# Switching to a transposing DMA one chunk earlier, with two scratch buffers per tensor and a reordered weight preparation

## The chip, the cores and the metric

The kernel runs on one core of one Trainium2 chip. The metric is the device time of that core in microseconds (us). A trace covers the span from the core's first to its last instruction, 1.7 to 2.2 us less than the device time in the runs of this study.

## The reference, cut to what matters

```python
# x, f_logit: 4 x 6144 x 256; w1, w2: 256 x 1024; w_out: 1024 x 256; all float32
sig = 1 / (1 + exp(-f_logit))
f = lower_bound + (1 - lower_bound) * sig
h = 0
for t in range(S):                    # a recurrence along the sequence
    h = f[:, t] * h + (1 - f[:, t]) * x[:, t]
    y[:, t] = h
out = maximum(y @ w1, y @ w2) @ w_out # 24576 tokens
```

## The kernel before

This kernel's matmuls take y with the feature dimension on the partitions, but f and x lie in memory with the tokens first. The sequence is cut into 26 chunks: four of 512 tokens at the start, then 22 of 1024. A block is 512 tokens, and there are 48. A chunk is turned in one of two ways. Early chunks are loaded with a cast to bf16 and transposed on TensorE. Later chunks are loaded into a DRAM scratch buffer with the same cast, and a transposing DMA brings them into SBUF.

```python
def by_xbar(c, s):                 # s = 0: f, s = 1: x
    return c >= (5, 6)[s]          # chunk index from which the DMA transposes
NSCR = 6                           # scratch buffers per tensor

def fetch(c):
    for s in range(2):
        ...                        # chunk 0 by the SyncE queue, cast on VectorE
        elif by_xbar(c, s):
            scr = scratch[s][uses[s] % NSCR]
            uses[s] += 1
            nc.gpsimd.dma_start(out=scr..., in_=src...)      # fp32 -> bf16
        else:
            nc.gpsimd.dma_start(out=nat..., in_=src...)      # to SBUF

def cross(c):
    for s in range(2):
        if by_xbar(c, s):
            nc.sync.dma_start_transpose(out=dst[:, :, 0:nt], in_=held[c, s][0:nt, :])
```

GpSimd does little but issue these loads, so it runs ahead of the computation until no scratch buffer is free: in the trace of before it issues them up to 40.81 us, and then waits 22.75 us for the first transposing DMA to free a buffer. SyncE issues the transposing DMAs and the outputs in program order.

The maximum is taken as a relu: wd is the scaled difference of w2 and w1, `first_layer` computes relu(wd.T y) with 16 matmuls of 512 columns, and `second_layer` multiplies that by w_out and adds y @ w13 with w13 = (scaled w1) @ w_out, 40 matmuls of 256 columns. The weight preparation before:

```python
def make_w1s(g):   # ScalarE: scaled copy of w1, fp32
    nc.scalar.mul(fcs(w1s, kc, g), half(w1n, g)[:, kc], om[:, kc:kc+1])
def make_wd(g):    # VectorE: w2 * om - w1s, 512 columns at a time
    nc.vector.scalar_tensor_tensor(out=fcs(wd, kc, g), in0=half(w2n, g)[:, kc], ...)
def make_w1T(k):   # TensorE transposes of w1s in fp32, ScalarE copies them to bf16
    ...
# order: make_w1s x2, make_wd(0), first_layer(0, 0..3), make_wd(1), make_w1T(0), (1),
#        first_layer(0, 4..7), make_w1T(2), (3), make_w13
```

The loop, cut to its order of work:

```python
LEAD_FETCH = 10; LEAD_CROSS = 3
for j in range(2, NBLK + 1):
    ahead("fetch", fetch, j + LEAD_FETCH)
    ahead("cross", cross, j + LEAD_CROSS)
    for fc in range(FC):
        if j < NBLK: first_layer(j, fc)
        second_layer(j - 1, fc)
        turn(...)          # TensorE transposes of block j + 2, if any
        ...                # gate (sigmoid) and scan of the next blocks
```

## Time and profile before

| what | value |
|---|---|
| device time, median of the first 3 runs | 409.04 us |
| span of the trace | 405.9 us |
| TensorE busy | 388.1 us, 96% |
| period of a block in the steady state | 7.82 us (48 blocks: 375 us) |
| first dense matmul stream | 14.05 us |
| first output matmul of block 0 | 23.92 us |
| first transposing DMA | issued 43.97, landed 63.5 us |

From the page of the kernel before: the busy times of the engines; the granted clock of TensorE and the mean busy share of the DMA engines in 40 slices of the span, in tenths; the chain of work that ended last, as shares by engine.

```profile
span 405.9 us, 7061 instructions
PE 388.1 (96%) x2792; PEld 297.3 (73%) x2840; DVE 247.2 (61%) x345; ACT 273.4 (67%) x446; POOL 28.0 (7%) x59
...
PEclk9999999999999999999999999999999999999999
DMA  7999999997999999897997995989772662752212
...
PE 82%; DMA 14%; issue 1%; SPq 0%; POOL 0%; ACT 0%; DVE 0%; ACTq 0%
```

TensorE is busy from end to end, and the chain is mostly TensorE. The DMA engines are full too for the first two thirds (mean share 0.85 to 1.20 in every stretch read between 10 and 300 us), but that alone does not say that anybody waited for them. Whether anybody did is in the list of what TensorE waited for (us in total, times, longest):

```profile
engine line waited for: us in total, times, longest us
PE dT L313 <- DVE wd L273: 5.6, 2, 5.2
PE tT L155 <- DVE fn L101: 2.8, 1, 2.8
...
PE dT L313 <- ACT rt L321: 1.2, 1, 1.2
```

The last line is a single wait of 1.2 us. The relus in front of it stood behind a sigmoid on ScalarE that had to wait for the first transposing DMA of f (2.7 us, until 63.6). SyncE's queue shows that DMA (start and duration of the issue):

```profile
...
30.05 13.82 SPq L365 DMA_DIRECT2D out_dram<-osb  x2
43.97 17.55 SPq L128 DMA_TRANSPOSE fT<-scr_0_90  x1
61.62 0.99 SPq L365 DMA_DIRECT2D out_dram<-osb  x2
```

Its issue alone took 17.55 us. The summary of the tile fT has its 19.6 us as the longest time from issue to landing:

```profile
DMA to landing us min/median/max: 4.7/5.9/19.6
```

The start, on TensorE alone (start, duration of the merged pieces, count):

```profile
start us, us, engine line op out<-in xcount [idle before <-releaser]
13.02 0.61 PE L313 MATMUL dT<-y,wd 128*128 128x512 bf16 x1 [5.17 <-DVE wd L273]
14.05 3.17 PE L313 MATMUL dT<-y,wd 128*128 128x512 bf16 x7 [0.42 <-DVE wd L273]
17.01 1.25 PE L287 MATMUL psO<-ident_f,w1s 128*128 128x128 f32 x8
18.09 1.98 PE L313 MATMUL dT<-y,wd 128*128 128x512 bf16 x8
...
20.79 2.41 PE L297 MATMUL psO<-wob,w1T 128*128 128x256 bf16 x16
...
23.92 0.27 PE L342 MATMUL psO<-w_117,y 128*128 128x256 bf16 x1
```

TensorE does nothing dense until 14.05. Then weight transposes (L287), the product w13 (L297) and transposes of block 1 (L155) stand between it and block 0's output matmuls (L342, at 23.92).

### The profile page before, as it was taken

To read this page: it belongs to the slowest core of one execution; us is meant where nothing else is said; L and a number is where in the kernel's file an instruction comes from. 1 tells how busy PE (TensorE), PEld (TensorE's weight loads), DVE (VectorE), ACT (ScalarE), POOL (GpSimd) and SP (SyncE) were. 2 spreads that over 40 slices of the span, in tenths; PEclk is the share of its full clock that TensorE was granted. 3 is DMA by queue.
4 is the path that set the end of the run, shared out by engine and by line. 5 is a ranking of instruction groups with operands and counts; after the bars stand their busy time and mean duration, and the time that the engine had idled before them with its cause. 6 is when DMAs were issued, how large, how long until landed. Compare 5 with 4: busy or idle time off the path is not lost.

```text
span 405.9 us, 7061 instructions
## 1 busy us (share of the span) xinstructions
PE 388.1 (96%) x2792; PEld 297.3 (73%) x2840; DVE 247.2 (61%) x345; ACT 273.4 (67%) x446; POOL 28.0 (7%) x59
## 2 busy tenths in 40 slices
PE   3699998999999999999999999999999999999996
PEld 2386776777777777777777777777777777777775
DVE  3557665676566567566656656756665665676641
ACT  2948655766766766676676677667667667766762
POOL 0721000000000000000000000000000000000000
PEclk9999999999999999999999999999999999999999
DMA  7999999997999999897997995989772662752212
GB/s 254 206 214 234 247 206 299 210 258 171 233 174 226 205 186 221 195 214 205 206 207 180 234 209 169 237 164 211 155 157 90 170 144 77 195 131 77 105 53 103
DMA packets 97568, 75.43 MB, mean 186 GB/s; under 512 B 87280, under 2 KB 87792, under 8 KB 96880
## 3 DMA queue, kind: packets, MB, share of 16 engines
q1 hardware_dynamic: 93984, 49.56, 47.7%
q0 software_dynamic: 3264, 25.17, 34.2%
q8 instruction: 22, 0.36, 0.4%
q10 hardware_dynamic: 288, 0.26, 0.2%
q14 instruction: 10, 0.08, 0.1%
HBM read 53.48 MB, written 46.66 MB: 247 GB/s over the span
## 4 chain that ended last, share of the span: by engine, by line
PE 82%; DMA 14%; issue 1%; SPq 0%; POOL 0%; ACT 0%; DVE 0%; ACTq 0%
PE psO L342 49%; PE dT L313 34%; DMA fT<-scr_0_90 5%; DMA scr_0_90<-in_f_logit_dram 4%; DMA scr_4_94<-in_f_logit_dram 3%; DMA w1n_118<-in_moe_w_dram 2%; DMA fn<-in_f_logit_dram 1%; POOL waited L269 0%; SPq L97 0%; ACT rt L321 0%; POOL wob L398 0%; SPq L380 0%; SPq L259 0%; DVE osb L351 0%; PE tT L155 0%
## 5 line engine op out<-in xcount | busy, mean ns | idle before, releaser
L321 ACT ACTIVATE rt<-dT 128x512 bf16<-128x512 f32 x384 | 223.3, 598 | 109.5 <-PE dT L313 93.4
L342 PE MATMUL psO<-wob,rt 128*128 128x256 bf16 x1536 | 229.1, 273 | 0.2
L313 PE MATMUL dT<-y,wd 128*128 128x512 bf16 x720 | 218.5, 382 | 6.9 <-DVE wd L273 5.6
L342 PEld LDWEIGHTS <-rt 128*128 128x128 bf16 x1536 | 170.0, 113 | 40.7
L362 DVE COPY osb<-psO 128x512 f32<-128x512 f32 x94 | 64.8, 691 | 76.2 <-PE psO L342 76.0
L208 DVE TENSOR_TENSOR_SCAN y<-ff,y,v 128x512 bf16<-128x512 bf16 x88 | 107.8, 1266 | 0.0
L313 PEld LDWEIGHTS <-wd 128*128 128x128 bf16 x768 | 73.9, 98 | 15.9 <-DVE wd L273 6.4
L342 PE MATMUL psO<-w_117,y 128*128 128x256 bf16 x384 | 73.3, 273 | 2.3
L342 PEld LDWEIGHTS <-y 128*128 128x128 bf16 x384 | 43.3, 113 | 41.0 <-issue 0.3
L195 DVE TENSOR_TENSOR v<-u,xT 128x1024 bf16<-128x1024 bf16 x40 | 27.7, 692 | 55.0 <-ACT u L165 55.0
L165 ACT ACTIVATE u<-fT 128x1024 bf16<-128x1024 bf16 x42 | 44.1, 1051 | 2.7 <-DMA fT<-scr_0_90 2.7
L184 DVE TENSOR_SCALAR ff<-u,nom 128x512 bf16<-128x512 bf16 x96 | 29.3, 347 | 0.0
L195 DVE TENSOR_TENSOR v<-u,tT 128x1024 bf16<-128x1024 bf16 x8 | 9.7, 1218 | 16.2 <-ACT u L165 14.9
L165 ACT ACTIVATE u<-tT 128x1024 bf16<-128x1024 bf16 x6 | 6.2, 1039 | 7.6 <-PE tT L155 7.5
L208 DVE TENSOR_TENSOR_SCAN y<-ff,v 128x512 bf16<-128x512 bf16 x8 | 9.3, 1206 | 0.0
L155 PE MATMUL tT<-ident,xn 128*128 128x128 bf16 x64 | 8.6, 230 | 0.3 <-DVE xn L101 0.3
L155 PE MATMUL tT<-ident,fn 128*128 128x128 bf16 x48 | 5.1, 234 | 2.8 <-DVE fn L101 2.8
L155 PEld LDWEIGHTS <-fn 128*128 128x128 bf16 x48 | 3.9, 105 | 3.5 <-DVE fn L101 3.1
L155 PEld LDWEIGHTS <-xn 128*128 128x128 bf16 x64 | 5.4, 103 | 0.6 <-DVE xn L101 0.6
L106 POOL DMA_DIRECT2D scr_0_90<-in_f_logit_dram x4 | 2.0, 496 | 50.0 <-DMA fT<-scr_0_90 49.4
L106 POOL DMA_DIRECT2D scr_2_92<-in_f_logit_dram x4 | 1.9, 487 | 37.0 <-DMA fT<-scr_2_92 36.2
L106 POOL DMA_DIRECT2D scr_1_91<-in_f_logit_dram x4 | 2.0, 495 | 36.4 <-DMA fT<-scr_1_91 35.8
(41 smaller groups left out, 49.4 us busy)
## 6 DMA issues: line engine op xcount, KB each, us to landing
out_dram<-osb SPq DMA_DIRECT2D x47, 512.0 KB, 3.6
scr_0_90<-in_f_logit_dram POOLq DMA_DIRECT2D x4, 512.0 KB, 6.9
scr_1_91<-in_f_logit_dram POOLq DMA_DIRECT2D x4, 512.0 KB, 6.2
scr_0_96<-in_x_dram POOLq DMA_DIRECT2D x4, 512.0 KB, 8.1
scr_2_92<-in_f_logit_dram POOLq DMA_DIRECT2D x4, 512.0 KB, 7.8
scr_1_97<-in_x_dram POOLq DMA_DIRECT2D x4, 512.0 KB, 8.4
scr_3_93<-in_f_logit_dram POOLq DMA_DIRECT2D x3, 512.0 KB, 6.7
scr_2_98<-in_x_dram POOLq DMA_DIRECT2D x3, 512.0 KB, 9.1
```

The source lines that it names most:

```text
L106: nc.gpsimd.dma_start(out=scr[0:nt, :].rearrange("(p i) d -> p (i d)", p=P), in_=src.rearrange("(p i) d -> p (i d)", p=P),)
L155: nc.tensor.transpose(dst, src, ident[:])
L165: nc.scalar.activation(out=like(u[:, :, 0:nb], src), in_=src, func=AF.Sigmoid, scale=-1.0)
L184: nc.vector.tensor_scalar(out=ff[:, h, 0:nb], in0=u[:, h, 0:nb], scalar1=nom[:, h : h + 1], scalar2=1.0, op0=ALU.mult, op1=ALU.add,)
L195: nc.vector.tensor_tensor(out=like(v[:, :, 0:nb], src), in0=like(u[:, :, 0:nb], src), in1=src, op=ALU.mult,)
L208: nc.vector.tensor_tensor_scan(out=y[:, h, 0:nb], data0=ff[:, h, 0:nb], data1=v[:, h, 0:nb], initial=init, op0=ALU.mult, op1=ALU.add,)
L313: nc.tensor.matmul(dT[:, 0:nb], lhsT=wd[:, kc, fc * P : (fc + 1) * P], rhs=y[:, kc, 0:nb], start=(kc == 0), stop=(kc == KC - 1),)
L321: nc.scalar.activation(out=rt[:, 0:nb], in_=dT[:, 0:nb], func=AF.Relu)
L342: nc.tensor.matmul(ps[:, r, :], lhsT=left, rhs=right, start=(s == 0 and (r == 0 or j == NBLK - 1)), stop=(s == n - 1 and (r == 1 or j == N ...
L362: nc.vector.tensor_copy(out=osb[:, 2 * g : 2 * g + 2, :], in_=ps[:])
```

## The change

Its intent is to take more transposes off TensorE, to shorten the start, and to keep the loads from running so far ahead. Its parts belong together. With two scratch buffers, the load of chunk c + 2 overwrites the buffer of chunk c, so in program order it must stand behind the transposing DMA that reads chunk c. That is why the lead goes from 10 blocks to 7 and `cross` moves ahead of `fetch`.

```diff
-        return c >= (5, 6)[s]
+        return c >= (4, 5)[s]
-    NSCR = 6
+    NSCR = 2
-    LEAD_FETCH = 10
+    LEAD_FETCH = 7
 ... weight preparation: difference first, then scale; transposes of the raw w1
-    def make_w1s(g): ...
+    def make_wd(k):
+        nc.vector.tensor_tensor(out=pair(wdf, k), in0=half(w2n, g)[:, :, qs],
+                                in1=half(w1n, g)[:, :, qs], op=ALU.subtract)
+        for kc in range(KC):
+            nc.scalar.mul(wd[:, kc, cols], wdf[:, kc, cols], om[:, kc : kc + 1])
+    def turn_w1(k): ...   # TensorE transposes of w1n instead of w1s
+    def keep_w1T(k, pt):
+        nc.vector.tensor_copy(out=dst, in_=pt[:])          # was ScalarE
-            nc.scalar.copy(out=w13[:, kc, :], in_=psw[:, 0, :])
+            nc.scalar.mul(w13[:, kc, :], psw[:, 0, :], om[:, kc : kc + 1])
 ... order at the start
+        pts = [turn_w1(0), turn_w1(1)]      # before any first_layer
+        make_wd(0); make_wd(1); first_layer(0, 0..1); keep_w1T(0, ...); ...
 ... loop
+            ahead("cross", cross, j + LEAD_CROSS)
             ahead("fetch", fetch, j + LEAD_FETCH)
-            ahead("cross", cross, j + LEAD_CROSS)
+            if j == 2:
+                for fc in range(FC):
+                    second_layer(1, fc)
             for fc in range(FC):
                 if j < NBLK: first_layer(j, fc)
-                second_layer(j - 1, fc)
+                if j > 2: second_layer(j - 1, fc)
```

(The added order line and the loop's conditions are shortened. The scan of block 2 also moves behind block 1's first layer in the text; nothing else on VectorE stands between the two places, so this changes nothing.)

More of the change, by code (lines that the diff above doesn't have):

```diff
@@ L238 @@
     wob = wpool.tile([P, FC, D], BF16)
-    w1s = wpool.tile([P, KC, DFF], FP32)
+    wdf = wpool.tile([P, KC, DFF], FP32)
     wd = wpool.tile([P, KC, DFF], BF16)
@@ L262, in fetch_w, with pair, turn_w1 @@
             )
-    def make_w1s(g):
-        for kc in range(KC):
-            nc.scalar.mul(fcs(w1s, kc, g), half(w1n, g)[:, kc], om[:, kc : kc + 1])
     def pool_waits(t):
         nc.gpsimd.tensor_copy(out=waited[:], in_=t)
-    def make_wd(g):
-        for kc in range(KC):
-            nc.vector.scalar_tensor_tensor(
-                out=fcs(wd, kc, g),
-                in0=half(w2n, g)[:, kc],
-                scalar=om[:, kc : kc + 1],
-                in1=fcs(w1s, kc, g),
-                op0=ALU.mult,
-                op1=ALU.subtract,
-            )
-    def make_w1T(k):
+    def pair(w, k):
+        return w[:, :, 2 * k * P : 2 * k * P + 2 * P].rearrange(
+            "p kc (q m) -> p kc q m", q=2
+        )
+    def make_wd(k):
+        g, r = divmod(k, NQ // 2)
+        qs = slice(2 * r, 2 * r + 2)
+        nc.vector.tensor_tensor(
+            out=pair(wdf, k), in0=half(w2n, g)[:, :, qs], in1=half(w1n, g)[:, :, qs],
+            op=ALU.subtract,
+        )
+        cols = slice(2 * k * P, 2 * k * P + 2 * P)
+        for kc in range(KC):
+            nc.scalar.mul(wd[:, kc, cols], wdf[:, kc, cols], om[:, kc : kc + 1])
+    def turn_w1(k):
+        g, r = divmod(k, NQ // 2)
         pt = ps_o.tile([P, KC, 2, P], FP32, name="psO")
@@ L285, in make_w1T @@
             for q in range(2):
-                fc = 2 * k + q
                 nc.tensor.transpose(
-                    pt[:, kc, q, :], w1s[:, kc, fc * P : (fc + 1) * P], ident_f[:]
+                    pt[:, kc, q, :], half(w1n, g)[:, kc, 2 * r + q], ident_f[:]
                 )
+        return pt
+    def keep_w1T(k, pt):
         dst = w1T[:, 2 * k : 2 * k + 2, :].rearrange("p q (k d) -> p k q d", k=KC)
-        nc.scalar.copy(out=dst, in_=pt[:])
+        nc.vector.tensor_copy(out=dst, in_=pt[:])
     def make_w13():
@@ L394 @@
         recurrence(0)
-        make_w1s(0)
-        make_w1s(1)
         pool_waits(w1n[0][:, 0, 0:1])
@@ L402 @@
         pool_waits(w2n[1][:, 0, 0:1])
-        make_wd(0)
-        for fc in range(0, NQ):
-            first_layer(0, fc)
         fetch(1)
@@ L409 @@
         ahead("fetch", fetch, LEAD_FETCH)
+        pts = [turn_w1(0), turn_w1(1)]
+        make_wd(0)
         make_wd(1)
-        make_w1T(0)
-        make_w1T(1)
-        for fc in range(NQ, FC):
+        for fc in range(0, 2):
             first_layer(0, fc)
-        make_w1T(2)
-        make_w1T(3)
+        keep_w1T(0, pts[0])
+        make_wd(2)
+        for fc in range(2, 4):
+            first_layer(0, fc)
+        make_wd(3)
+        keep_w1T(1, pts[1])
+        pts = [turn_w1(2), turn_w1(3)]
+        for fc in range(4, 6):
+            first_layer(0, fc)
+        keep_w1T(2, pts[0])
+        for fc in range(6, 8):
+            first_layer(0, fc)
+        keep_w1T(3, pts[1])
         make_w13()
@@ L422 @@
         turn(turn_steps(2))
-        recurrence(2)
+        gate(2)
         for fc in range(FC):
             first_layer(1, fc)
+        for step in scan_steps(2):
+            step()
         turn(turn_steps(3))
@@ L440 @@
                     first_layer(j, fc)
-                second_layer(j - 1, fc)
+                if j > 2:
+                    second_layer(j - 1, fc)
                 n = len(steps)
```

## The prediction

> **What bounds it now.** TensorE: busy 388 of 405.9 us at granted clock 1.00 (the page's busy times), 82% of the chain of waits. In the timeline a block of 16 N=512 and 40 N=256 matmuls has a period of 7.82 us (97.16, 104.97, 112.80). 48 blocks make 375 us; only about 30 us are anything else: the start (no dense matmul before 14.05 us), weight preparation on TensorE (16 fp32 transposes and 16 matmuls between 17.0 and 23.0, about 4 us), 112 activation transposes, one stall of 1.24 us at 64 us (list of waits), the tail. VectorE (61%) and ScalarE (67%) are hidden. DMA engines are full (share about 1.0) up to 150 us because loads run far ahead into 12 scratch buffers; that delays only the first transposing DMA, issued at 43.97, landed at 63.5 (6 us is typical), which makes the 1.24 us stall.
>
> **What the change does.**
> 1. Transposes. f of blocks 4,5 and x of blocks 6,7 leave TensorE: 32 transposes. A slot of the loop with two takes 1.09 us, with one 1.03, with none 0.978: 0.055 us each, **-1.8 us**, on the critical path.
> 2. Start. The first 16 fp32 transposes of w1 need only the raw w1 (landed at 9.97) and run in idle TensorE time at 10 to 14 us. [...]block 0's first-layer matmuls were issued 0.43 us apart from 14.05 to 17, later about half that[...]. Against it ScalarE gets 8 scalings (estimated from a 0.37 us copy of 256 columns: 0.4 to 0.46 us each) on top of 8 relus (0.6 us), and ends the preparation at about 21. Block 0's output matmuls start at about 21.7, not 23.9: **-2.2 us** (1 to 3).
> 3. The stall at 64 us goes: with 2 buffers about 7 large loads stand before the first transposing DMA, not 15. **-1.2 us.**
> 4. Un-interleaving block 2: its first layer runs alone, paced by relus, and the scan of block 3 starts only after block 1's output copies. **+0.8 us** (0 to 1.5).
> 5. Steady state: unchanged. A scratch buffer is refilled when its transposing DMA has landed; the load lands in 6 to 9 us and has about 31 us. DMA work is the same, spread evenly (before: share 0.95 early, 0.3 at the end).
>
> Sum: -4.4 us.
>
> **The risk.** Chunk 4's f now needs load to scratch, then a transposing DMA issued at about 28 us behind block 0's output, needed at about 40. Up to three 512 KB loads may still be queued then, each about 2.9 us of all engines (34.2% of the span for about 48.5), so I expect landing at 34 to 37. If it is starved as at 44 us (19.6 us), TensorE stalls about 5 us and the gain is gone.
>
> **Predicted: 404.6 us**, 402.0 to 408.5. Faster by over 2%: 0.04; within 2%: 0.91; slower by over 2%: 0.05.
>
> **To check afterwards.** Activation transposes 80, not 112; fp32 transposes from about 10 us; block 0's output matmuls at 21 to 22.5; no wait behind an fT transposing DMA; period still 7.82; GpSimd waits for a transposing DMA twice per 15.6 us; DMA share flat at about 0.8 into the last fifth.
>
> **What would make it wrong.** A late first or second fT; two buffers that turn into a chain load, transpose, load longer than 15.6 us per chunk; or strided fp32 reads of raw weights that make VectorE the limit of the start (its weight groups took 1.1 us per 512 columns).

The sum: -1.8 - 2.2 - 1.2 + 0.8 = -4.4 us, from 409.0 to 404.6.

## The result

After: 403.66 us, median of 4 runs (403.42 to 404.54), against 408.92 us (408.33 to 409.08, 4 runs). The ratio is 0.9878, with a 95% interval of 0.9859 to 0.9897. Ratios here are the mean time of one kernel's fast runs over that of the other's fast runs of the same rounds, so they are not quite the ratios of the medians quoted. The gain of 1.2% is clear of noise.

The page after, the same lines:

```profile
span 402.8 us, 7010 instructions
PE 387.5 (96%) x2760; PEld 296.9 (74%) x2808; DVE 248.8 (62%) x349; ACT 269.7 (67%) x446; POOL 27.4 (7%) x59
...
PEclk9999999999999999999999999999999999999999
DMA  7999989899799998899997999996996989953212
...
PE 94%; DVE 3%; DMA 1%; issue 1%; SPq 0%; ACT 0%; DVEq 0%
```

The DMA share no longer falls off at two thirds of the span; it holds until the last loads are in (0.96 between 300 and 350 us, against 0.58 before). What TensorE waited for:

```profile
...
PE psO L288 <- DMA w1n_110<-in_moe_w_dram: 2.4, 1, 2.4
...
PE dT L317 <- ACT wd L281: 1.3, 1, 1.3
PE dT L317 <- DVE y L208: 0.7, 1, 0.7
```

The wait for a relu is gone. A wait of 0.7 us for y is new. SyncE's queue and the summary of fT:

```profile
...
29.52 0.36 SPq L369 DMA_DIRECT2D out_dram<-osb  x1
29.99 6.84 SPq L128 DMA_TRANSPOSE fT<-scr_0_90  x1
38.59 0.37 SPq L369 DMA_DIRECT2D out_dram<-osb  x1
39.05 2.50 SPq L128 DMA_TRANSPOSE fT<-scr_1_91  x1
```

```profile
DMA to landing us min/median/max: 5.0/6.2/10.4
```

The first transposing DMA is now issued at 29.99 and takes the longest again, but it is 10.4 us and it is in time. The start on TensorE:

```profile
start us, us, engine line op out<-in xcount [idle before <-releaser]
10.28 1.95 PE L288 MATMUL psO<-ident_f,w1n_110 128*128 128x128 f32 x8 [2.37 <-DMA w1n_110<-in_moe_w_dram]
13.57 3.59 PE L317 MATMUL dT<-y,wd 128*128 128x512 bf16 x8 [1.33 <-ACT wd L281]
16.95 1.91 PE L288 MATMUL psO<-ident_f,w1n_111 128*128 128x128 f32 x8
18.66 0.63 PE L317 MATMUL dT<-y,wd 128*128 128x512 bf16 x1
...
20.74 1.91 PE L301 MATMUL psO<-wob,w1T 128*128 128x256 bf16 x16
...
23.38 0.38 PE L346 MATMUL psO<-w_109,y 128*128 128x256 bf16 x2
```

The weight transposes (now L288) begin at 10.28 in idle time, but block 0's output matmuls (now L346) start only 0.54 us earlier than before: 23.38 against 23.92. The two traces differ by 3.1 us of span, the timed runs by 5. So the first pair of traces alone does not explain the gain.

### The profile page after: what moved, and what is told of

Its sections match the earlier page's. It is cut to its first block, busy times and chain, and to the rows that moved or that the text cites. A ratio compares the mean times of both kernels' runs of the same rounds, so it can differ in the third digit from the quotient of the medians.

```text
span 402.8 us, 7010 instructions
## 1 busy us (share of the span) xinstructions
PE 387.5 (96%) x2760; PEld 296.9 (74%) x2808; DVE 248.8 (62%) x349; ACT 269.7 (67%) x446; POOL 27.4 (7%) x59
## 3 DMA queue, kind: packets, MB, share of 16 engines
q0 software_dynamic: 2784, 25.17, 36.6%
## 4 chain that ended last, share of the span: by engine, by line
PE 94%; DVE 3%; DMA 1%; issue 1%; SPq 0%; ACT 0%; DVEq 0%
PE psO L346 54%; PE dT L317 38%; DMA x_124<-in_x_dram 1%; PE tT L155 1%; DVE y L208 1%; DVE v L195 1%; PE psO L301 0%; PE psO L288 0%; DVE ff L184 0%; DVE wdf L275 0%; DVE xn L101 0%; DVE osb L366 0%; ACT wd L281 0%; SPq L384 0%; SPq L97 0%
## 5 line engine op out<-in xcount | busy, mean ns | idle before, releaser
L346 PE MATMUL psO<-wob,rt 128*128 128x256 bf16 x1536 | 228.4, 273 | 2.3
L317 PE MATMUL dT<-y,wd 128*128 128x512 bf16 x720 | 217.9, 382 | 2.3 <-ACT wd L281 1.3
L346 PEld LDWEIGHTS <-rt 128*128 128x128 bf16 x1536 | 169.9, 113 | 39.9
L317 PEld LDWEIGHTS <-wd 128*128 128x128 bf16 x768 | 74.8, 98 | 11.5 <-issue 2.5
L346 PE MATMUL psO<-w_109,y 128*128 128x256 bf16 x384 | 73.3, 273 | 0.1
L346 PEld LDWEIGHTS <-y 128*128 128x128 bf16 x384 | 43.1, 113 | 40.8 <-issue 1.0
L195 DVE TENSOR_TENSOR v<-u,xT 128x1024 bf16<-128x1024 bf16 x42 | 29.1, 692 | 57.8 <-ACT u L165 57.8
L165 ACT ACTIVATE u<-fT 128x1024 bf16<-128x1024 bf16 x44 | 46.2, 1049 | 0.0
L106 POOL DMA_DIRECT2D scr_0_90<-in_f_logit_dram x11 | 5.4, 493 | 136.6 <-DMA fT<-scr_0_90 136.6
L106 POOL DMA_DIRECT2D scr_1_91<-in_f_logit_dram x11 | 5.4, 488 | 127.5 <-DMA fT<-scr_1_91 127.0
L195 DVE TENSOR_TENSOR v<-u,tT 128x1024 bf16<-128x1024 bf16 x6 | 7.3, 1220 | 9.3 <-ACT u L165 8.1
L165 ACT ACTIVATE u<-tT 128x1024 bf16<-128x1024 bf16 x4 | 4.2, 1048 | 7.6 <-PE tT L155 7.6
L281 ACT ACTIVATE wd<-wdf,om 128x256 bf16<-128x256 f32 x8 | 3.6, 503 | 5.5 <-DVE wdf L275 5.4
L106 POOL DMA_DIRECT2D scr_0_92<-in_x_dram x11 | 5.4, 487 | 19.9 <-DMA xT<-scr_0_92 19.2
L155 PE MATMUL tT<-ident,xn 128*128 128x128 bf16 x48 | 6.4, 234 | 0.3 <-DVE xn L101 0.3
L106 POOL DMA_DIRECT2D scr_1_93<-in_x_dram x10 | 4.9, 487 | 13.0 <-DMA xT<-scr_1_93 13.0
L155 PE MATMUL tT<-ident,fn 128*128 128x128 bf16 x32 | 2.9, 242 | 2.9 <-DVE fn L101 2.9
```

Of the source, the lines that this page charges most:

```text
L106: nc.gpsimd.dma_start(out=scr[0:nt, :].rearrange("(p i) d -> p (i d)", p=P), in_=src.rearrange("(p i) d -> p (i d)", p=P),)
L155: nc.tensor.transpose(dst, src, ident[:])
L165: nc.scalar.activation(out=like(u[:, :, 0:nb], src), in_=src, func=AF.Sigmoid, scale=-1.0)
L195: nc.vector.tensor_tensor(out=like(v[:, :, 0:nb], src), in0=like(u[:, :, 0:nb], src), in1=src, op=ALU.mult,)
L281: nc.scalar.mul(wd[:, kc, cols], wdf[:, kc, cols], om[:, kc : kc + 1])
L317: nc.tensor.matmul(dT[:, 0:nb], lhsT=wd[:, kc, fc * P : (fc + 1) * P], rhs=y[:, kc, 0:nb], start=(kc == 0), stop=(kc == KC - 1),)
```

## The experiments

All eleven runs gave correct results. They were made in three groups. The kernel before ran beside them: medians 408.27, 408.41 and 408.48 us in the three groups. Four of its runs, from 424.8 to 435.6 us, were slow (mean granted clock 0.984 to 0.994; the others 0.998 to 1.000) and are set aside.

**1. Both kernels again.** No edit.

> The kernel before, run again as it is, for the noise and for a second trace. The profile of before that the prediction was made from is 1 us shorter than its timed runs (408.0 against 409.0), and the profile of after is 1 us longer than its timed runs (404.5 against 403.4), so the profiles differ by 3.1 us of span and the timed runs by 5.0. Theory (run-to-run luck in the start and at the first transposing DMA): ratio 1.000 within 0.002, and in this trace the start of block 0's output matmuls (23.92) or the stall at 64 us (1.24) differs by up to 1 us from the first trace. Rival (the difference is something systematic that a profile hides): this trace repeats 23.92 and 1.24 within 0.1 us.

> The kernel after, run again as it is. Theory [...]: ratio 0.988 (403.6 to 404.4 us), and the fp32 transposes at 17 us and the first-layer matmuls up to 19.4, which ran at half rate in the first trace, may run at full rate in this one, with block 0's output matmuls up to 1 us earlier than 23.38. Rival: [...]half rate up to about 19 us again, output matmuls at 23.4 within 0.2.

Before again: 408.15 us, ratio 0.9995 (0.9979 to 1.0011). After again: 403.42 us, ratio 0.9881 (0.9866 to 0.9896). The second traces differ from the first at the start, as the theory of luck has it. In before, block 0's output matmuls moved from 23.92 to 24.75; in after, from 23.38 to 22.18. The reason is visible in the second trace of after (TensorE, same columns):

```profile
16.73 1.11 PE L288 MATMUL psO<-ident_f,w1n 128*128 128x128 f32 x8
...
22.18 0.38 PE L346 MATMUL psO<-w,y 128*128 128x256 bf16 x2
```

The eight fp32 transposes (L288) took 1.91 us at 16.95 in the first trace and take 1.11 us here. In both traces of after, first-layer matmuls are issued 0.42 to 0.43 us apart up to 17 us and 0.22 us apart later; the instant at which TensorE goes from the half rate to the full one differs from run to run. The granted clock does not show this: it reads 1.00 in every microsecond from 13 to 17 us of the first traces of before and after, while the matmuls are issued 0.42 to 0.43 us apart. Why the rate changes is not shown. From 22.18 to 397.06, the start of the last group of L346 matmuls, this trace takes 374.88 us, and the first one (23.38 to 398.26) takes 374.88 us as well. All of the difference between them is the start.

One trace of each kernel is therefore too few for the start. Over all traces, block 0's output matmuls begin at 23.92, 24.75, 24.62 and 24.68 with the old weight preparation (mean 24.49). With the new one and no filler they begin at 23.38, 22.18, 22.21, 22.90, 22.58, 23.36 and 22.37 (mean 22.71). The reordering is worth about **1.8 us**, not 0.54; the two sets do not overlap, but each scatters by about a microsecond.

**2. The transposing-DMA part alone.**

```diff
 (on before)
-        return c >= (5, 6)[s]
+        return c >= (4, 5)[s]
-    NSCR = 6 ; LEAD_FETCH = 10
+    NSCR = 2 ; LEAD_FETCH = 7
 (and cross ahead of fetch)
```

> Before with the transposing-DMA part alone: f by DMA from the fifth chunk and x from the sixth, two scratch buffers per tensor, fetch lead 7, transposes issued ahead of fetches; weight preparation and block 2 as before. Theory (terms of the prediction): -1.8 for 32 transposes and -1.2 for the stall, so 406.0 us, ratio 0.9927. Rival (the gain is mostly the weights and the clock): under 1.5 us gained, ratio over 0.9963.

404.68 us, ratio 0.991 (0.9893 to 0.9926), so 3.7 us gained; no wait for a relu is left. The rival is out: this part carries most of the gain. It gains somewhat more than the 3.0 expected. The traces give a steadier measure, from block 0's output matmuls to the start of the last group of L342 or L346 matmuls, as used in experiment 1: 377.37 and 377.03 us in the two traces of before, 374.18 here, so 2.9 to 3.2 us less.

**3. Two scratch buffers alone.**

```diff
 (on before)
-    NSCR = 6 ; LEAD_FETCH = 10
+    NSCR = 2 ; LEAD_FETCH = 7
 (and cross ahead of fetch)
```

> Before with two scratch buffers per tensor, fetch lead 7 and transposes issued ahead of fetches, but still f from the sixth chunk and x from the seventh, and the old weight preparation. Theory (depth of the prefetch is what starved the first transposing DMA, and the stall is all that it cost): the first fT lands within 10 us of its issue instead of 19 to 22, no wait of TensorE for a relu near 64 us, 0.9 to 1.3 us gained, about 407.1 us, ratio 0.997; the other 2.4 us of the transposing-DMA part (ratio 0.991 measured) are then the 32 transposes (1.8) and a rest. Rival (two buffers cost something in the steady state, which the fewer transposes paid for): no gain or a loss, ratio 1.000 or more, with waits spread over the span.

407.11 us, ratio 0.996 (0.9944 to 0.9977): 1.6 us. SyncE's queue at the first fT, and the summary of fT:

```profile
44.73 2.72 SPq L128 DMA_TRANSPOSE fT<-scr  x1
...
DMA to landing us min/median/max: 4.7/5.3/6.7
```

The first fT is issued at 44.73, when the last queued load has landed (at 40.99), and no fT takes over 6.7 us to land. The wait of TensorE for a relu is gone, and none has come in its place. (The lead and the order came along in this edit; experiments 5 and 6 vary the buffers alone.) Two buffers cost nothing in the steady state: from block 8 to block 40 every trace takes 250.24 us. The step from here to experiment 2 is 0.005 of 408.4 us, about 2.0 us (1 to 3 by the intervals), for 32 transposes expected at 1.8. The stretch of experiment 2 takes 375.97 us here and 374.18 there: **1.79 us**. Against the two traces of before, the stall is worth 1.1 to 1.4 us in it.

**4. The weight part alone.**

```diff
 (on after: everything back to before, except the weight preparation)
-        return c >= (4, 5)[s]        # back to (5, 6)
-    NSCR = 2 ; LEAD_FETCH = 7        # back to 6 and 10, fetch ahead of cross
-            if j == 2: ...           # back to interleaved layers
```

> Before with the reordered weight preparation alone, and block 2 interleaved as before; scratch, leads and transposes as before. Theory (first trace of after: output matmuls at 23.38 instead of 23.92): -0.5 us, ratio 0.9988; the stall at 64 us may grow by as much, since the first transposing DMA does not land earlier, and then nothing is gained: ratio 0.999 to 1.000. Rival (the prediction's step 2): -2.2 us, ratio 0.9946.

This came out worse than either theory. The three fast runs took 408.44, 411.41 and 412.12 us: ratio 1.0057 (1.0018 to 1.0095). The other three, 416.8 to 445.2 us, were slow (granted clock 0.969 to 0.992) and are left out. The trace (of a fast run) shows a start as good as any, with output matmuls at 22.21, and then this wait of TensorE:

```profile
PE dT L317 <- ACT rt L325: 4.0, 1, 4.0
```

The first transposing DMA is issued 1.7 us earlier than in before (42.28 against 43.97). It takes 22.3 us instead of 19.6, so it lands no earlier: its landing is set by the loads, not by its issue. TensorE, ahead by 1.7 us, waits 4.0. The stretches around the wait show what the clock did (busy time and count of each engine, granted clock, DMA share, GB/s):

```profile
core 0: us, PE busy (x) PEld busy (x) DVE busy (x) ACT busy (x) POOL busy (x), PEclk, DMA share, GB/s
60.00:65.00 5.00, 2.29 (x19) 1.70 (x17) 0.00 (x0) 0.30 (x1) 0.00 (x0) 0.96 1.08 259
65.00:70.00 5.00, 3.49 (x14) 2.04 (x15) 4.21 (x6) 3.38 (x6) 0.96 (x2) 0.50 2.38 265
```

The granted clock drops to 0.50 after the wait. From block 0's output matmuls to the last group this trace takes 382.63 us, 6.66 more than experiment 3, where nobody waits: 4.0 are the wait, and the other 2.6 come with the slow clock (the first two first-layer matmuls behind the wait take 1.01 us, the two before it 0.59). Against before, the sum is -1.7 for the start, +2.8 for the longer wait and about +2.5 for the clock, and the two spans do differ by 3.6 us (409.5 and 405.9). So the wait alone costs more than the start gained here, and the clock comes on top. The three fast runs are not alike, though: two, this trace's run among them, had a mean granted clock of 0.991, and the one of 408.44 us had 0.998 and lost nothing against before. The loss of 0.6% is a mean over both kinds.

**5. After with six buffers.**

```diff
 (on after)
-    NSCR = 2
+    NSCR = 6
```

> After with six scratch buffers per tensor instead of two, nothing else changed. Theory (loads ahead of need starve the transposing DMA; two buffers are what makes the earlier switch possible): the first fT, issued at about 29 us, lands only when the run of loads ends, estimated from 16 loads of 2.9 us after 13.5 us at 50 to 60 us, needed at about 42: a stall of 10 us or more, TensorE's clock throttled after it, 414 us or more, ratio over 1.012. Rival (the transposing DMA was late in before because it was issued late, behind block 1's output at 44[...]): lands by 42 us, under 405 us, ratio under 0.992.

419.92 us, ratio 1.0285 (1.026 to 1.031). The wait of TensorE, and the summary line of fT (the first fT is the longest):

```profile
PE dT L317 <- ACT rt L325: 13.2, 1, 13.2
```

```profile
DMA to landing us min/median/max: 4.7/5.7/28.2
```

Issued at 29.19, the first transposing DMA lands 28.2 us later, at 57.4, within the estimated 50 to 60. The rival, that it was late in before because it was issued late, is out. What starves it is the loads that GpSimd has queued: wherever loads were still queued when the first fT was issued, it landed 1.6 to 4.5 us after the last of them. That load landed at 55.71 here and fT at 57.42; in before at 61.90 and 63.53, in after at 35.91 and 40.44, and in experiment 2 at 34.43 and 37.71, though its fT was issued 1.2 us later than that of after. How the DMA engines divided their time between the loads and fT is not shown. On the page of before a packet of the loads is 7.7 KB (25.17 MB in 3264) and one of SyncE's queue 0.5 KB, outputs included (49.56 MB in 93984); no run shows whether that has a part in the lateness. TensorE stood still for 13.2 us, and the granted clock fell to 0.50 again.

**6. After with three buffers.**

```diff
 (on after)
-    NSCR = 2
+    NSCR = 3
```

> After with three scratch buffers per tensor, a point between two (no stall) and six (13.2 us). Two more 512 KB loads of 2.9 us each stand beside the first transposing DMA. Theory ([...]every load adds its time): fT lands about 5.7 us later than the 37 to 41 of after, at 44 to 46, needed at about 42: a stall of 2 to 4 us, 406 us, ratio about 0.995. Rival (a threshold elsewhere, such as waits of the loads for each other): the stall is 0 as with two, or over 8 as with six.

404.09 us, ratio 0.989 (0.9872 to 0.9908). The first fT took 13.6 us to land, at 43.6, against 10.4 and 12.2 us in the two traces of after, and 28.2 with six buffers. The expected stall of 2 to 4 us did not come. I overestimated the step in the landing: 1.4 to 3.2 us for two more loads, not 5.7. The end of the loads did move about as expected, from 35.91 and 36.78 to 41.20, but fT then landed 2.4 us after it instead of 4.2 to 4.5. (In the other traces of this start with two buffers the slowest fT took 11.5 to 12.6 us, so a single trace with three is not far outside the scatter.) ScalarE took fT up at 43.70, at once, and TensorE waited for no relu. Its start was late (23.36), as in the first trace of after, so this time cannot be told apart from after. Three buffers are just enough in this trace, and the slack is used up.

**7. After with block 2's layers interleaved again.**

```diff
 (on after)
-            if j == 2:
-                for fc in range(FC):
-                    second_layer(1, fc)
...
-                if j > 2:
-                    second_layer(j - 1, fc)
+                second_layer(j - 1, fc)
```

> After, with block 2's first layer interleaved again with block 1's second layer, as in before. Theory (step 4 of the prediction: relus pace the lone first layer, and the scan of block 3 comes late, seen as the wait of 0.7 us for y before block 3): 0.4 to 0.8 us faster than after: 402.8 us, ratio 0.9865. Rival (y of block 2 is then not ready when TensorE reaches it, and the first transposing DMA is needed earlier): no gain or up to 1 us slower than after, with a wait for y or for fT instead.

403.32 us, ratio 0.9871 (0.9852 to 0.9889): not resolved from after by time. The traces are steadier than the times here. From block 0's first output matmul to block 2's, after takes 19.47 us in both of its traces (23.38 to 42.85, 22.18 to 41.65), and this kernel takes 18.79 (22.90 to 41.69). Block 2's first output matmuls, and the wait for y before them, in after:

```profile
42.64 0.38 PE L317 MATMUL dT<-y,wd 128*128 128x512 bf16 x1 [0.69 <-DVE y L208]
42.85 0.38 PE L346 MATMUL psO<-w_109,y 128*128 128x256 bf16 x2
```

And in this kernel:

```profile
41.69 0.38 PE L346 MATMUL psO<-w,y 128*128 128x256 bf16 x2
```

The wait for y is gone. So taking the layers apart costs **0.7 us**, as step 4 of the prediction had it; this trace's start was 0.7 us later than that of after again, which hides it.

**8. After with TensorE kept busy at the start.**

```diff
 (on after)
-        for q in range(8):
+        for q in range(32):
             nc.tensor.transpose(wt[:, 0:P], ident[:], ident[:])
         turn(turn_steps(0))
+        for q in range(22):
+            nc.tensor.transpose(wt[:, 0:P], ident[:], ident[:])
...
         pts = [turn_w1(0), turn_w1(1)]
+        for q in range(14):
+            nc.tensor.transpose(wt[:, 0:P], ident[:], ident[:])
```

> After, with 24, 22 and 14 more throw-away 128-column transposes of the identity on TensorE in its idle stretches before 5.4, from 8 to 10.3 and from 12.3 to 13.5 us, so that it is busy without a gap. Theory [...]: first-layer matmuls of block 0 0.22 us apart from 13.5 us, block 0's output matmuls at 21.3 to 21.8 instead of 22.2 and 23.4, about 1 us faster than after on average: 402.4 us, ratio 0.986, and less scatter. Rival (ScalarE and VectorE pace the start[...]): output matmuls no earlier than 22.1, 403.4 us.

402.83 us, ratio 0.9861 (0.9842 to 0.988), and its four runs lie within 0.6 us. TensorE at the start (L413 is the filler):

```profile
start us, us, engine line op out<-in xcount [idle before <-releaser]
10.14 1.20 PE L288 MATMUL psO<-ident_f,w1n 128*128 128x128 f32 x8 [1.39 <-DMA w1n<-in_moe_w_dram]
11.17 0.94 PE L413 MATMUL dT<-ident 128*128 128x128 bf16 x14
13.20 2.46 PE L317 MATMUL dT<-y,wd 128*128 128x512 bf16 x8 [1.08 <-ACT wd L281]
15.49 1.11 PE L288 MATMUL psO<-ident_f,w1n 128*128 128x128 f32 x8
...
21.66 0.38 PE L346 MATMUL psO<-w,y 128*128 128x256 bf16 x2
```

Block 0's first eight first-layer matmuls (L317) take 2.46 us instead of 3.59 and 3.40. The output matmuls start at 21.66, earlier than in any trace without the filler. TensorE is not busy without a gap, as was intended: it still idles 1.39 us before the transposes and 1.08 us before the first-layer matmuls. The gain over after is about 0.6 to 0.8 us by the medians; the runs do not overlap (402.67 to 403.24 against 403.31 to 404.54), but the intervals of the two ratios do. It is less than the 1 us expected, though the start of this trace is 1.05 us earlier than the mean of 22.71. ScalarE's scalings and relus follow each other without a wait from 12.63 to 20.01 us, so they pace the start here; in the first trace of after ScalarE waited 1.0 us for TensorE. The rate of TensorE, as in the theory, and the pace of ScalarE, as in the rival, each have a part.

**9. x from the fifth chunk as well.**

```diff
 (on after)
-        return c >= (4, 5)[s]
+        return c >= (4, 4)[s]
```

> After, with x too by DMA from the fifth chunk, so 16 transposes fewer on TensorE. Theory (0.055 us for each transpose as long as the DMA keeps its deadline): the second transposing DMA, for x of chunk 4, lands at about 45, and VectorE wants it at 43.5, so TensorE waits 1 us or less for y of block 4 and nothing or up to 0.9 us is gained: 402.6 to 403.6 us, ratio 0.986 to 0.989. Rival (one more transposing DMA and one more load to scratch push f of chunk 4 past its deadline): a stall for fT, over 404.5 us.

403.23 us, ratio 0.9878 (0.9859 to 0.9897): no gain over after is resolved. The deadline of f is kept, as there is no wait for a relu, but the wait for y before block 3 is still there (0.8 us). The eight transposes saved in block 2's lone first layer lie in a stretch that relus and that wait pace; the other eight are worth 0.4 us by the estimate of 0.055 each, below what the times resolve. The traces do show it: from block 0's output matmuls to the last group 374.43 us, against 374.88 in both traces of after.

**10. Filler and interleaving together.** The edits of 7 and 8.

> After with both: the throw-away transposes that keep TensorE busy at the start, and block 2's layers interleaved again. In the traces the distance from block 0's to block 2's first output matmul is 19.47 us in after and 18.79 with the layers interleaved, so interleaving is worth 0.7, though the timed runs did not resolve it (403.4 against 403.3, with a start that was 0.7 us later). Theory (the two add up[...]): 402.1 us, ratio 0.9845, output matmuls of block 0 at 21.7. Rival (the first transposing DMA, needed 1 us earlier, becomes the limit): 402.8 us or more, and a wait of TensorE for a relu or of ScalarE for fT near 41 us.

402.1 us, median of 402.04 to 402.47, ratio 0.9847 (0.9832 to 0.9862). It is as expected, and the best kernel: 1.3 us faster than after again, with no wait for a relu or for y in its trace.

## Why the prediction was right, and where it was not

The predicted 404.6 us lies 0.9 us from the measured 403.66, inside 402.0 to 408.5. Point by point:

1. **Transposes, -1.8.** Right. Activation transposes are 80 instead of 112. The step from two buffers alone to the whole DMA part is about 2.0 us in the timed runs and 1.79 in the traces.
2. **Start, -2.2.** Nearly right in size: -1.8 as a mean over traces. The reasons given were partly wrong. "The first 16 fp32 transposes" are 8: there are 16 in all, and the other 8 stay between first-layer matmuls. And an effect on TensorE's rate, which the prediction gave them too, did not show: block 0's first-layer matmuls were still about 0.43 us apart. The idle stretch of TensorE from 12.2 to 13.6 may have a part in that, but it is not shown to: in experiment 8 TensorE idles there too (1.08 us), and the matmuls behind it are 0.22 us apart. There the eight transposes before the gap already ran at nearly the full rate (1.20 us, not 1.95). The gain is what the table of the start shows: 8 transposes out of the busy stretch, first-layer matmuls that run without a break from 13.57 instead of 14.05, and copies that no longer hold up w13 (1.91 us instead of 2.41). These three came together, and no run takes them apart. Experiment 8 shows that filling TensorE's idle time at the start does help: block 0's first eight first-layer matmuls then took 2.46 us instead of 3.59 and 3.40. That the size came out is partly luck: output matmuls "at 21 to 22.5" missed in the first trace (23.38), and the 23.92 that the prediction started from is the earliest of the four starts with the old preparation.
3. **Stall, -1.2.** Right in cause, shown by experiments 3 and 5; the waits are 1.2 and 0.9 us in the two traces of before; the timed runs of experiment 3 give about 1.6 (0.9 to 2.3 by the interval).
4. **Lone layers, +0.8.** Right: 0.7 by the traces of experiment 7.
5. **Steady state unchanged.** Right: two blocks' output groups lie 7.82 us apart (93.15 and 100.97 in the chain of after). GpSimd waits twice for each chunk, as foretold (12.79 and 1.38 us before the loads at 82.14 and 84.00). The DMA share is flat, but at 0.94 to 0.97 between 100 and 350 us, not 0.8.

The risk was sized too kindly. The first fT landed at about 40 to 41, not 34 to 37. It was in time because it was needed at 43.5 (42.3 in the second trace), not at 40. That two misses cancel is luck. The slack is 1.3 to 3 us (0.9 in the trace of experiment 9), and in the one trace with a third buffer it was used up. The danger named last, VectorE as the limit of the start, came in part: ScalarE's first scaling waits until 13.0 us for VectorE's first difference, which begins at 11.93, behind block 0's scan (a difference of 512 columns took 1034 to 1064 ns in the trace of after), and TensorE then waits 1.3 us for the scaling.

The terms as measured in traces (-1.8, -1.8, -1.2 or -0.9, +0.7) make -3.8 to -4.1 us; the timed runs make -4.9 (0.0119 of 408.3). Part of the rest lies outside the span: device time minus span is 2.06 us in the profiled run of before again, and 1.74 in that of after again. About half a microsecond stays open, which is no more than the interval of the ratio leaves (0.6 us either way).

The parts do not add freely. The weight part is worth 1.8 us at the start, yet alone it loses 0.6% (experiment 4), since the time it gains is spent waiting for a DMA whose landing does not move, and since the granted clock fell after that wait (to 0.50 in the trace; 0.991 as the mean of two of its three fast runs). With the DMA part in place, the same code is a gain: from 0.991 to 0.9871 in the interleaved version.

## What to carry to other kernels

A queue of loads that runs as far ahead as its buffers allow was not free here: the next urgent DMA on another queue landed only after those loads (1.6 to 4.5 us after the last of them), so give a prefetch the depth that its deadline needs and no more. Before shortening a start, find the first transfer that the shortened start will meet earlier, and ask whether that transfer can land earlier too. When a kernel's start varies by more than the effect that you look for (22.18 and 23.38 us here, with identical code), compare stretches of several traces between the same two instructions, not one span with another.
